# Seven block products instead of eight in the first products of two fused ffn layers

## The chip, the cores and the metric

The kernel runs on one core of one Trainium2 chip. The time is that of the whole kernel on the device, in microseconds; the median of three runs before the change is 671.86 us (671.8 to 671.88).

## The reference

Three blocks follow each other, all in float32 on arrays that are given in wider types where they are weights (64-bit, read as two 32-bit words):

```python
q_pool = q.reshape(B, H, S // 2, 2, D).mean(axis=3)        # B=2, H=8, S=1152, D=64
scores = (1 / sqrt(D)) * q_pool @ k.T
attn   = softmax(scores)
x      = (attn @ v) as [B * 576, 512]                       # 1152 tokens of 512
h = x @ w_in1                                               # 512 -> 2048
g = where(h >= 1, h, where(h <= -1, 0, (h + 1)**2 / 4))
x = g @ w_out1                                              # 2048 -> 512
h = x @ w_in2;  g = h * sigmoid(h);  out = g @ w_out2       # the second layer, same sizes
```

## The kernel before, in words

**Precision.** Every matrix that TensorE multiplies is split into a high part (rounded to fp32r) and a low part (what is left). A product of two such matrices is three matmuls: high x high, high x low, low x high. ScalarE makes the high parts with a copy; `lo_of` (L145) subtracts them for the low parts, nearly always on GpSimd (POOL).

**Weights.** `weight_tasks` (L85) loads a tile of 128 x 512 weights over SyncE's queue (SP) and turns its two words into float32 in five stages: `size` (L110, ScalarE), then `clamp` (L115), `shift` (L119), `sign` (L123) and `rest` (L127) on VectorE (DVE). All stages work in SBUF, on the tile `wf`, except for the first eight tiles, which are converted during attention by way of a PSUM bank. Then ScalarE copies the high part and GpSimd subtracts the low part.

**Ffn.** The 16 tiles of 128 hidden features of a layer are taken in groups of four (`GF`), the 1152 tokens in three blocks of 384 (`TB`). A step is one feature tile and one token block; there are 48 steps in a layer. `gemm1` (L158) makes the hidden values of a step: 4 chunks of 128 of x, three matmuls each, 12 matmuls of 384 columns, into one of four banks. Layer one: VectorE clips (L178), ScalarE squares (L184), VectorE takes the maximum (L188). Layer two: ScalarE's sigmoid (L180), then VectorE multiplies (L188). ScalarE copies the high part `gh` (L194), GpSimd makes the low part `gl`. `gemm2` (L202) multiplies by the output weights three steps later (`AHEAD`): in layer one 12 matmuls of 384 columns (L210), in layer two 9 of 512 (L212). Four banks add up the four tiles of a group. `keep` (L218) then takes a bank out: ScalarE copies it for the first group, VectorE adds it to `part` (L224) for the others. After the last group of layer one `part_hi` and `part_lo` split the sums for layer two; after that of layer two they are stored.

**The order.** Nothing is scheduled by a compiler. Every operation is an `op` with a target time, a list of engines with an estimate of how long it takes (occupied, and until its result is there), what it depends on, and the buffers that it needs. `plan_out` (L281) plays this through and always issues, on the engine that can start first, the operation that can start first; equal ones by target time. Targets are moved by a random amount (`SEED`, `SPREAD`). The program order of each engine comes from there and is fixed then. `both=True` marks VectorE operations that the planner keeps apart from GpSimd's. Attention's operations, the first eight weight tiles and the first steps of the ffn are in the same plan, so that ffn matmuls fill the end of attention.

Of the kernel before, what the change touches and what calls it, by code (L numbers as in the profile page):

```python
# [19 lines left out]
def fused_kernel(  # L20
# [16 lines left out]
    P = 128  # L37
# [7 lines left out]
    GF = 4  # L45
    NG = NF // GF
    FG = GF * P
    SC = S // 3
    RAWS, EARLY_RAWS = 4, 2
# [8 lines left out]
    SEED, SPREAD = 10, 1.0  # L58
    AHEAD = 3.0
# [3 lines left out]
    WPACE = 1.5  # L63
# [18 lines left out]
    seq = [(layer, g) for layer in range(2) for g in range(NG)]  # L82
    wt = {}

    def weight_tasks(idx, kind, pools, RAWS, via):  # L85


        layer, g = seq[idx]
        src = (((w_in1, w_out1), (w_in2, w_out2))[layer])["io".index(kind)]
        raws, parts = pools  # L90

        def quarter(c):
            st = {}

            def load():
                if c == 0:
                    wt[layer, g, kind] = [
                        parts.tile([P, 4, 512], F32R, tag=f"w{x}{kind}", name=f"w{x}{kind}") for x in "hl"
                    ]
                if kind == "i":  # L100
                    sv = src[c * P : (c + 1) * P, g * FG * 2 : (g + 1) * FG * 2]
                else:
                    sv = src[g * FG + c * P : g * FG + (c + 1) * P, :]
                raw = raws.tile([P, 512, 2], U32, tag="wr", name="wr", bufs=RAWS)
                nc.sync.dma_start(out=raw.rearrange("p f w -> p (f w)"), in_=sv)
                st["low"], st["top"] = raw[:, :, 0], raw[:, :, 1]

            def size():
                st["w"] = raws.tile([P, 512], F32, tag="wf", name="wf", bufs=RAWS)
                nc.scalar.activation(st["w"], st["top"].bitcast(F32), AF.Abs)  # L110

            def clamp():

                st["x"] = via[c]() if c in via else st["w"]
                nc.vector.tensor_scalar(st["x"], st["w"], LEAST, MOST, ALU.max, ALU.min)  # L115

            def shift():
                xi = st["x"].bitcast(U32)
                nc.vector.tensor_scalar(xi, xi, 3, 0x3FFFFFF8, ALU.logical_shift_left, ALU.bitwise_and)  # L119

            def sign():
                xi = st["x"].bitcast(U32)
                nc.vector.scalar_tensor_tensor(xi, st["top"], 0xC0000000, xi, ALU.bitwise_and, ALU.bitwise_or)  # L123

            def rest():
                wi, xi = st["w"].bitcast(U32), st["x"].bitcast(U32)
                nc.vector.scalar_tensor_tensor(wi, st["low"], 29, xi, ALU.logical_shift_right, ALU.bitwise_or)  # L127

            def parts_of():
                hi, lo = wt[layer, g, kind]  # L130
                nc.scalar.copy(hi[:, c], st["w"])
                lo_of(nc.gpsimd, lo[:, c], st["w"], hi[:, c])

            def part_hi():
                nc.scalar.copy(wt[layer, g, kind][0][:, c], st["w"])  # L135

            def part_lo():
                lo_of(nc.gpsimd, wt[layer, g, kind][1][:, c], st["w"], wt[layer, g, kind][0][:, c])

            return load, size, clamp, shift, sign, rest, parts_of, part_hi, part_lo  # L140

        return [quarter(c) for c in range(4)]
# [3 lines left out]

# [5 lines left out]
    TB = 384  # L152
    NB = NT // TB
    steps = [(layer, g, tb, j) for layer, g in seq for tb in range(NB) for j in range(GF)]
    hps, gg = {}, {}
    act = None

    def gemm1(i, ps, half):  # L158

        layer, g, tb, j = steps[i]  # L160
        wh, wl = wt[layer, g, "i"]
        ts_ = slice(tb * TB, (tb + 1) * TB)
        for c in range(half * ND // 2, (half + 1) * ND // 2):
            for n, (w, a) in enumerate(((wh, xh), (wh, xl), (wl, xh))):
                nc.tensor.matmul(  # L165
                    ps,
                    lhsT=w[:, c, j * P : (j + 1) * P],
                    rhs=a[:, c, ts_],
                    start=(c == 0 and n == 0),
                    stop=(c == ND - 1 and n == 2),  # L170
                )
        hps[i] = ps

    def act_a(i):
        gf = act.tile([P, TB], F32, tag="gf", name="gf")
        gg[i] = gf
        if steps[i][0] == 0:
            nc.vector.tensor_scalar(gf, hps[i], -1.0, 1.0, ALU.max, ALU.min)  # L178
        else:
            nc.scalar.activation(gf, hps[i], AF.Sigmoid)  # L180

    def act_b(i):
        if steps[i][0] == 0:
            nc.scalar.activation(gg[i], gg[i], AF.Square, bias=0.5, scale=0.5)  # L184

    def act_c(i):
        gf = gg[i]
        nc.vector.tensor_tensor(gf, hps.pop(i), gf, op=ALU.mult if steps[i][0] else ALU.max)  # L188

    def act_d(i):  # L190
        gf = gg[i]
# [5 lines left out]
    def act_e(i):  # L197
        gh, gl, gf = gg[i]
        lo_of(nc.gpsimd, gl, gf, gh)
        gg[i] = (gh, gl)  # L200
# [36 lines left out]

    part1 = part2 = None

    booked = []
# [758 lines left out]
```

## Time and profile before

| | |
|---|---|
| median of the runs | 671.86 us |
| the profiled execution's own time | 672.01 us |
| its span, first to last instruction | 670.2 us |
| TensorE busy (PE) | 663.2 us, 99% |
| weight loads of TensorE (PEld) | 619.9 us, 92% |
| VectorE (DVE) | 514.5 us, 77% |
| GpSimd (POOL) | 435.9 us, 65% |
| ScalarE (ACT) | 419.1 us, 63% |
| granted TensorE clock | 0.999 |

A share is a mean over three stretches that differ: attention to about 260 us, layer one to about 468 us, layer two to the end. Ends of matmuls are modelled and overlap with the next start; the distance between starts is what a matmul takes in a row.

### The profile page before, as it was taken

To read this page: it belongs to the slowest core of one execution; us is meant where nothing else is said; L and a number is where in the kernel's file an instruction comes from. 1 tells how busy PE (TensorE), PEld (TensorE's weight loads), DVE (VectorE), ACT (ScalarE), POOL (GpSimd) and SP (SyncE) were. 2 spreads that over 40 slices of the span, in tenths; PEclk is the share of its full clock that TensorE was granted. 3 is DMA by queue.
4 is the path that set the end of the run, shared out by engine and by line. 5 is a ranking of instruction groups with operands and counts; after the bars stand their busy time and mean duration, and the time that the engine had idled before them with its cause. 6 is when DMAs were issued, how large, how long until landed. Compare 5 with 4: busy or idle time off the path is not lost.

```text
span 670.2 us, 11784 instructions
## 1 busy us (share of the span) xinstructions
PE 663.2 (99%) x3962; PEld 619.9 (92%) x3962; DVE 514.5 (77%) x1184; ACT 419.1 (63%) x808; POOL 435.9 (65%) x413
## 2 busy tenths in 40 slices
PE   8999999999999999999999999999999999999997
PEld 7899998999899989999999999999999998989996
DVE  7888989898988897388898987886873684983223
ACT  6989998989999887455635543545554543432221
POOL 5888998989899689455645553576763653553121
PEclk9999999999999999999999999999999999999999
DMA  8967676666544455114233232221232231200012
GB/s 250 293 203 226 204 195 198 207 206 200 180 144 155 161 190 172 60 64 127 94 125 97 96 119 69 95 74 56 100 117 60 98 95 50 103 5 0 1 48 94
DMA packets 55292, 84.29 MB, mean 126 GB/s; under 512 B 14784, under 2 KB 32832, under 8 KB 55232
## 3 DMA queue, kind: packets, MB, share of 16 engines
q1 hardware_dynamic: 54656, 83.12, 39.5%
q8 instruction: 31, 0.51, 0.3%
q10 hardware_dynamic: 576, 0.43, 0.2%
q14 instruction: 29, 0.24, 0.1%
HBM read 49.81 MB, written 2.39 MB: 78 GB/s over the span
## 4 chain that ended last, share of the span: by engine, by line
PE 93%; DVE 4%; ACT 1%; issue 1%; DMA 1%; ACTq 0%; DVEq 0%
PE bank L165 30%; PE bank L210 15%; PE bank L212 15%; PE bank L613 11%; PE bank L690 10%; PE bank L677 5%; PE bank L732 2%; DVE p L620 2%; PE bank L673 2%; PE bank L501 1%; PE bank L719 1%; PE bank L537 1%; DMA kraw<-in_k_dram 1%; DVE thl L652 0%; DVE part L224 0%
## 5 line engine op out<-in xcount | busy, mean ns | idle before, releaser
L145 POOL TENSOR_TENSOR gl<-gf,gh 128x384 fp32r<-128x384 f32 x96 | 108.9, 1136 | 122.4 <-ACT gh L194 111.0
L165 PE MATMUL bank<-xh,whi 128*128 128x384 f32 x384 | 129.7, 338 | 0.0
L165 PE MATMUL bank<-xl,whi 128*128 128x384 f32 x384 | 129.2, 336 | 0.0
L165 PE MATMUL bank<-xh,wli 128*128 128x384 f32 x384 | 129.2, 336 | 0.0
L620 DVE TENSOR_SCALAR_CACHE_REDUCE p<-bank 128x384 f32<-128x384 f32 x192 | 102.1, 552 | 15.2 <-PE bank L613 11.4
L690 PE MATMUL bank<-thl,vhl 128*128 128x512 f32 x288 | 109.7, 421 | 0.0
L188 DVE TENSOR_TENSOR gf<-bank,gf 128x384 f32<-128x384 f32 x96 | 53.0, 552 | 73.7 <-ACT gf L180 69.2
L145 POOL TENSOR_TENSOR thl<-pf,thl 128x512 fp32r<-128x512 f32 x80 | 103.1, 1295 | 1.6
L613 PE MATMUL bank<-kk,qm 128*128 128x384 f32 x384 | 95.8, 352 | 0.4
L633 ACT ACTIVATE p<-p,low 128x1152 f32<-128x1152 f32 x64 | 81.4, 1273 | 2.6 <-DVE low L630 2.2
L194 ACT CAST gh<-gf 128x384 fp32r<-128x384 f32 x96 | 49.4, 514 | 48.4 <-DVE gf L188 42.7
L180 ACT ACTIVATE gf<-bank 128x384 f32<-128x384 f32 x48 | 23.6, 491 | 82.5 <-PE bank L165 81.3
L165 PEld LDWEIGHTS bank<-xh,whi 128*128 128x128 f32 x384 | 72.1, 188 | 3.1
L165 PEld LDWEIGHTS bank<-xl,whi 128*128 128x128 f32 x384 | 72.1, 188 | 3.0
L165 PEld LDWEIGHTS bank<-xh,wli 128*128 128x128 f32 x384 | 72.1, 188 | 0.0
L613 PEld LDWEIGHTS bank<-kk,qm 128*128 128x128 f32 x384 | 65.3, 189 | 5.5 <-DVE thl L652 0.5
L145 POOL TENSOR_TENSOR wlo<-wf,who 128x512 fp32r<-128x512 f32 x32 | 44.0, 1376 | 37.8 <-ACT who L135 34.5
L210 PE MATMUL bank<-gh,who 128*128 128x384 f32 x192 | 65.0, 339 | 0.0
L210 PE MATMUL bank<-gh,wlo 128*128 128x384 f32 x192 | 64.9, 338 | 0.0
L210 PE MATMUL bank<-gl,who 128*128 128x384 f32 x192 | 64.8, 337 | 0.0
L145 POOL TENSOR_TENSOR wli<-wf,whi 128x512 fp32r<-128x512 f32 x32 | 44.2, 1382 | 30.4 <-ACT whi L135 30.3
L652 DVE TENSOR_TENSOR thl<-bank,thl 128x512 fp32r<-128x512 f32 (+1 forms) x88 | 56.4, 649 | 4.9 <-ACT thl L651 4.2
(98 smaller groups left out, 1542.7 us busy)
## 6 DMA issues: line engine op xcount, KB each, us to landing
pr<-p SPq DMA_DIRECT2D x64, 256.0 KB, 2.8
wr<-in_moe_w_in_dram SPq DMA_DIRECT2D x32, 512.0 KB, 3.7
wr<-in_moe_w_out_dram SPq DMA_DIRECT2D x32, 512.0 KB, 3.3
pr<-p SPq DMA_DIRECT2D x64, 192.0 KB, 2.7
vraw<-in_v_dram SPq DMA_DIRECT2D x16, 288.0 KB, 3.0
kraw<-in_k_dram SPq DMA_DIRECT2D x15, 288.0 KB, 3.9
qraw<-in_q_dram SPq DMA_DIRECT2D x15, 256.0 KB, 3.9
rb<-row SPq DMA_DIRECT2D x16, 128.0 KB, 3.3
```

Source lines behind the costliest of these rows:

```text
L145: eng.tensor_sub(out, whole, hi.bitcast(F32))
L165: nc.tensor.matmul(ps, lhsT=w[:, c, j * P : (j + 1) * P], rhs=a[:, c, ts_], start=(c == 0 and n == 0), stop=(c == ND - 1 and n == 2),)
L188: nc.vector.tensor_tensor(gf, hps.pop(i), gf, op=ALU.mult if steps[i][0] else ALU.max)
L194: nc.scalar.copy(gh, gf)
L210: nc.tensor.matmul(ps[:, :TB], lhsT=w[:, j, m * P : (m + 1) * P], rhs=a, start=start, stop=stop)
L212: nc.tensor.matmul(ps[:, cols], lhsT=a[:, m * P : (m + 1) * P], rhs=w[:, j, cols], start=start, stop=stop)
L613: nc.tensor.matmul(ps, lhsT=qq[:, c0 : c0 + P], rhs=rhs, start=n == 0, stop=n == last)
L620: nc.vector.tensor_scalar(dst, ps, -1.0, None, ALU.mult, ALU.min, accum_out=mxs[key, t][:, j : j + 1])
L633: nc.scalar.activation(pt(), pt(), AF.Exp, bias=lows[key][:, tt : tt + 1], scale=-1.0, accum_out=sums[key][:, tt : tt + 1])
L652: o2 = op(target + 0.3, ("DVE", 0.6 * f, 0.683 * f, lambda: nc.vector.tensor_sub(tl(), ps(), th().bitcast(F32))), [o1], [bank, tb])
L677: nc.tensor.transpose(banks[bank.slot][:, i * P : (i + 1) * P].bitcast(F32R), prs[x][:, i, (c - COPIED[x][0]) * P : (c + 1 - COPIED[x][0]) ...
L690: nc.tensor.matmul(banks[yb.slot], lhsT=lhsT, rhs=thls[tb.slot][i], start=not count, stop=len(count) == 2 * KC - 1)
```

## The change

The whole ffn is written anew, with the same precision. Feature tiles are taken in 8 pairs `p` per layer, tokens in two blocks `SB`: 512 tokens in halves of 256, and 640 in halves of 320. A unit is a layer, a pair and a block. In the units of `PLAIN` (pairs 0 to 3 and 7 of layer one, 0 to 2 of layer two) the first product is made as before, in 24 matmuls of 512 columns or 48 of 320. In the other 8 pairs the product of a 2 x 2 block matrix of weights (two halves of x's features by the two tiles) and a 2 x 2 block matrix of x (two halves of its features by the two halves of the tokens) is made with seven products of six matmuls each instead of eight.

For that, weights need four more blocks, sums and differences of theirs (`combine`, on VectorE, 128 columns each, for each of the two loaded halves) with high and low parts of their own, and x needs four differences per token block and layer (`differences`). Where two products go to one sum, the second is added to the first in its PSUM bank (`start` is set for products 1, 6 and 5 alone): products 1 and 2 in bank 6, products 6, 7 and 4 in bank 4, products 5 and 3 in bank 5. VectorE takes sums out of the banks in between (five additions per unit), ScalarE copies twice; a product that adds to a bank waits until the bank was read (`reads`). Of these units the activation then works from SBUF, over both halves at once. The low parts `gl` of the hidden values are on GpSimd alone.

Weights are loaded and converted in the same number of tiles. The later stages of a conversion now go by way of PSUM bank 7 (`shift`, `sign`, `rest`); `clamp` stays in SBUF. Banks 0 to 3 add up the second products; where two units in a row share a token block, four of the block's keys (column tiles) are added over both and taken out once. In the last unit the keys are closed one after the other. Random shifts of targets have another seed, and a smaller width after attention.

```diff
...
-    SEED, SPREAD = 10, 1.0
-    AHEAD = 3.0
+    SEED, LATE_SEED, SPREAD, LATE_SPREAD = 24, 4, 1.0, 0.3
+    NP = NF // 2
+    SB = ((0, 256), (512, 320))
+    PLAIN = tuple((l, p, sb) for l in range(2) for p in range(NP) for sb in range(2) if (l, p) not in ((0, 4), (0, 5), (0, 6), (1, 3), (1, 4), (1, 5), (1, 6), (1, 7)))
+    LAG, LAGS = 1.2, {(0, 7): 0.0}
+    LEAD, RAW_I = 22, 2
+    TWINS, SHARED = ((0,0),(1,0)), ((1,0),)
...
+    def stages(raw, wf, bank, far):
+        low, top = raw[:, :, 0], raw[:, :, 1]
+        u = lambda x: x.bitcast(U32)
+        def size():
+            nc.scalar.activation(wf, top.bitcast(F32), AF.Abs)
+        def clamp():
+            nc.vector.tensor_scalar(bank if far else wf, wf, LEAST, MOST, ALU.max, ALU.min)
+        def shift():
+            nc.vector.tensor_scalar(u(bank), u(bank if far else wf), 3, 0x3FFFFFF8, ALU.logical_shift_left, ALU.bitwise_and)
+        def sign():
+            nc.vector.scalar_tensor_tensor(u(bank), top, 0xC0000000, u(bank), ALU.bitwise_and, ALU.bitwise_or)
+        def rest():
+            nc.vector.scalar_tensor_tensor(u(wf), low, 29, u(bank), ALU.logical_shift_right, ALU.bitwise_or)
+        return size, clamp, shift, sign, rest
...
+            rnd, late = Random(SEED), Random(LATE_SEED)
+            for n, o in enumerate(ops):
+                r = rnd if n < count else late
+                o.target += r.uniform(-SPREAD, SPREAD) * (1.0 if n < count else LATE_SPREAD)
...
+            flat = limit == 2 and not far
+            bank = None if flat else Buf("b") if far else Buf("b", want=7)
...
+            o = op(target, ("ACT", 0.57, 0.672, f(0)), [o], [raw])
+            if far:
+                o = op(target + 0.3, ("DVE", 0.6, 0.69, f(1)), [o], [raw, bank])
+            else:
+                o = op(target + 0.3, ("DVE", 0.332, 0.42, f(1)), [o], [raw], both=True)
+            for m in (2, 3, 4):
+                way = ("DVE", 0.335, 0.427) if flat and m == 2 else ("DVE", 0.6, 0.69)
+                o = op(target + 0.3 * m, (*way, f(m)), [o], [raw] if flat else [raw, bank], both=flat)
...
+                def combine(m, e, sf=sf, wf=wf):
+                    w, s = wf().rearrange("p (b n) -> p b n", n=P), at_(sf)
+                    add, sub = e.tensor_add, e.tensor_sub
+                    if m == 0:
+                        add(s[:, 0], w[:, 1], w[:, 3])
+                    elif m == 1:
+                        sub(s[:, 1], s[:, 0], w[:, 0])
+                    elif m == 2:
+                        sub(s[:, 2], w[:, 0], w[:, 1])
                     else:
...
+                        sub(s[:, 3], w[:, 2], s[:, 1])
+                for m in range(4):
+                    f = lambda e, m=m, c=combine: lambda: c(m, e)
+                    o = op(t + 1.8, [("DVE", 0.2, 0.29, f(nc.vector))], [o, *then], [raw, sf], both=True)
...
+        units = []
+        for layer in range(2):
+            p, last = 0, 1
+            while p < NP:
+                some = [p, p + 1] if (layer, p) in TWINS else [p]
+                first = last if p else 1 - last
+                units += [(layer, x, sb) for sb in (first, 1 - first) for x in some]
+                p, last = p + len(some), 1 - first
...
+            for m, (n, needs, a, b) in enumerate(((0, None, (0, 1), (0, 0)), (1, 0, (1, 1), None), (3, 1, (1, 0), None), (2, None, (1, 1), (0, 1)))):
+                steps = [("tensor_sub", n, (None, *a), b and (None, *b))]
+                if layer == 0:
+                    steps = [("tensor_sub", n, (xh, *a), b and (xh, *b)), ("tensor_add", n, None, (xl, *a)), ("tensor_sub", n, None, b and (xl, *b))]
...
+        def product(wb, block, rhs, ps, first):
+            wh, wl = at_(wb)
+            mh, ml = rhs
+            for i in range(2):
+                for n, (w, a) in enumerate(((wh, mh), (wh, ml), (wl, mh))):
+                    nc.tensor.matmul(ps, lhsT=w[:, i, block], rhs=a[:, i], start=first and i == n == 0, stop=i == 1 and n == 2, skip_group_check=not first)
...
+                what = [(0, "B11"), (2, "B21"), (7, "B22"), (3, "T4"), (4, "T1"), (5, "T2"), (6, "T3")]
+                size = 6 * MM[w]
+                o_c, reads = {}, {}
+                held = [Buf("b", want=6), Buf("b", want=4), Buf("b", want=5)]
+                for k, (m, x, dst, src) in enumerate(((1, 0, (0, 0), None), (6, 1, (0, 1), (0, 0)), (5, 2, None, None), (7, 1, (1, 1), (0, 0)), (2, 0, None, None), (4, 1, (1, 0), (0, 0)), (3, 2, (0, 1), (0, 1)))):
+                    bank = held[x]
+                    block, rhs = what[m - 1]
+                    tk = t + span * k / 7
+                    first = m in (1, 6, 5)
+                    go = lambda bank=bank, block=block, rhs=rhs, first=first: product(wb, block, blocks_of(u, rhs), bank_of(bank)[:, :w], first)
+                    o = after("PE", op(tk, ("PE", size, size + 0.165, go), [*deps, before.get("PE"), reads.get(x)], [bank, wb]))
+                    def add(dst, src, x, o, *needs, tk=tk):
+                        f = lambda: nc.vector.tensor_add(h_of(*dst), bank_of(held[x])[:, :w], h_of(*src))
+                        o_c[dst] = reads[x] = op(tk + size, ("DVE", *dve(w), f), [o, o_c[src], *needs], [held[x], hb[dst[0]], hb[src[0]]])
+                    if m == 1:
+                        f = lambda: nc.scalar.copy(h_of(0, 0), bank_of(held[0])[:, :w])
+                        o_c[0, 0] = reads[0] = op(tk + size, ("ACT", *act(w), f), [o], [held[0], hb[0]])
+                    elif m == 5:
+                        fifth = o
+                    elif m == 2:
+                        second_ = o
+                    else:
+                        add(dst, src, x, o)
+                        if m == 7:
+                            add((1, 1), (1, 1), 2, fifth)
+                f = lambda: nc.scalar.copy(h_of(0, 0), bank_of(held[0])[:, :w])
+                o_c[0, 0] = op(t + span, ("ACT", *act(w), f), [second_, o_c[1, 0]], [held[0], hb[0]])
+                ready = [[o_c[0, 0], o_c[0, 1]], [o_c[1, 0], o_c[1, 1]]]
...
+                        f = lambda s=s, hh=hh: nc.vector.scalar_tensor_tensor(hh(), s(), 1.0, hh(), ALU.min, ALU.max)
+                    else:
+                        o = op(t1, ("ACT", *act(n2), lambda s=s, hh=hh: nc.scalar.activation(s(), hh(), AF.Sigmoid)), ready[jj], bufs)
+                        f = lambda s=s, hh=hh: nc.vector.tensor_mul(hh(), hh(), s())
+                    o = op(t1 + 1, ("DVE", *dve(n2), f), [o], bufs, both=True)
...
+                ways = [("POOL", *pool_(n2), f)]
+                if True:
+                    if False: ways = [("DVE", *dve(n2), lambda gh=gh, gl=gl, hh=hh: lo_of(nc.vector, gl(), hh(), gh()))]
...
+            joined = n - 1 in opens
+            joins = same(n + 1) and not joined
+            if joins:
+                opens.add(n)
+            keys = keys_of[layer][sb]
+            shared = keys[-4:]
+            solo = keys[:-4]
+            final = n + 1 == len(units)
+            lots = [shared, solo] if joined else [solo, shared]
+            if final:
+                lots = [[k] for k in keys]
...
+                        closes = jj == 1 and not (joins and key in shared)
...
```

## Rows read from the trace of the kernel before

**Rows 1.** The profile's page, busy time, share and instructions.
```profile
PE 663.2 (99%) x3962; PEld 619.9 (92%) x3962; DVE 514.5 (77%) x1184; ACT 419.1 (63%) x808; POOL 435.9 (65%) x413
```

**Rows 2.** Busy time by stretch; PE, PEld, DVE, ACT, POOL, clock, DMA share, GB/s.
```profile
20.00:260.00 240.00, 239.24 (x1683) 219.07 (x1682) 212.59 (x683) 222.18 (x433) 215.46 (x218) 1.00 0.63 195
273.50:468.00 194.50, 194.49 (x1109) 194.13 (x1108) 162.40 (x257) 95.98 (x181) 106.53 (x87) 1.00 0.28 87
468.00:650.00 182.00, 182.00 (x914) 164.77 (x913) 110.36 (x160) 75.91 (x146) 86.67 (x72) 1.00 0.19 63
...
300.00:350.00 50.00, 49.99 (x286) 49.68 (x285) 45.55 (x70) 26.58 (x51) 27.71 (x23) 1.00 0.33 106
```

**Rows 3.** Longest wait of TensorE: total us, times, longest.
```profile
PE bank L426 <- POOL thl L408: 1.5, 1, 1.5
```

**Rows 4.** Timeline of TensorE in layer one: start, duration, instruction.
```profile
401.15 0.34 PE L210 MATMUL bank<-gh,who 128*128 128x384 f32 x1
...
403.27 0.34 PE L165 MATMUL bank<-xh,whi 128*128 128x384 f32 x1
...
405.38 0.34 PE L210 MATMUL bank<-gh,who 128*128 128x384 f32 x1
```

**Rows 5.** Chain that ended last, in layer two: start, us, what.
```profile
625.34 2.09 PE bank L165 x12
627.43 2.10 PE bank L212 x9
```

**Rows 6.** Timeline of the end, all engines (q is an issue).
```profile
664.95 2.17 DVE L224 TENSOR_TENSOR part<-bank,part 128x512 f32<-128x512 f32 x4 [3.78 <-PE bank L212]
...
665.46 0.28 PE L212 MATMUL bank<-who,gh 128*128 128x256 f32 x1
...
665.58 0.28 PE L212 MATMUL bank<-who,gl 128*128 128x256 f32 x1
...
666.05 0.28 PE L212 MATMUL bank<-wlo,gh 128*128 128x256 f32 x1
667.16 0.35 ACTq L236 DMA_DIRECT2D out_dram<-part  x1
```

**Rows 7.** Timeline of VectorE in layer two.
```profile
655.04 0.55 DVE L188 TENSOR_TENSOR gf<-bank,gf 128x384 f32<-128x384 f32 x1
655.50 1.28 DVE L224 TENSOR_TENSOR part<-bank,part 128x512 f32<-128x512 f32 x2
```

**Rows 8.** VectorE by line and shape, whole span: busy, mean ns | idle before.
```profile
L123 DVE SCALAR_TENSOR_TENSOR wf<-wr,wf 128x512 uint32<-128x512 uint32 x56 | 55.8, 996 | 0.7
...
L127 DVE SCALAR_TENSOR_TENSOR wf<-wr,wf 128x512 uint32<-128x512 uint32 x56 | 54.3, 970 | 0.7
...
L119 DVE TENSOR_SCALAR wf<-wf 128x512 uint32<-128x512 uint32 x56 | 37.5, 669 | 0.6
L115 DVE TENSOR_SCALAR wf<-wf 128x512 f32<-128x512 f32 x56 | 37.1, 663 | 1.2 <-ACT wf L110 1.1
...
L224 DVE TENSOR_TENSOR part<-bank,part 128x384 f32<-128x384 f32 x36 | 18.6, 547 | 1.2 <-PE bank L210 1.2
L224 DVE TENSOR_TENSOR part<-bank,part 128x512 f32<-128x512 f32 x26 | 17.6, 688 | 15.8 <-PE bank L212 15.7
...
L123 DVE SCALAR_TENSOR_TENSOR bank<-wr,bank 128x512 uint32<-128x512 uint32 x8 | 5.5, 688 | 0.0
L127 DVE SCALAR_TENSOR_TENSOR wf<-wr,bank 128x512 uint32<-128x512 uint32 x8 | 5.5, 683 | 0.1
...
L224 DVE TENSOR_TENSOR part<-bank,part 128x256 f32<-128x256 f32 x2 | 0.8, 421 | 0.0
```

**Rows 9.** GpSimd by line and shape, 300 to 400 us.
```profile
L145 POOL TENSOR_TENSOR gl<-gf,gh 128x384 fp32r<-128x384 f32 x24 | 28.8, 1199 | 21.5 <-ACT gh L194 13.1 <-issue 8.2
L145 POOL TENSOR_TENSOR wlo<-wf,who 128x512 fp32r<-128x512 f32 x10 | 14.3, 1427 | 11.5 <-ACT who L135 11.5
L145 POOL TENSOR_TENSOR wli<-wf,whi 128x512 fp32r<-128x512 f32 x10 | 14.2, 1424 | 11.9 <-ACT whi L135 11.9
```

More of the change, by code (lines that the diff above doesn't have):

```diff
@@ L79, in fused_kernel @@
     xl = const.tile([P, ND, NT], F32R, name="xl")
-    seq = [(layer, g) for layer in range(2) for g in range(NG)]
     wt = {}
[L85 to L142, printed above, removed]
@@ L151, in fused_kernel @@
     wpre = ctx.enter_context(tc.tile_pool(name="wpre", bufs=1, side="right"))
[L152 to L188, printed above, removed]
@@ L249, in __init__, with fits @@
             if due is not None:
                 booked.append(self)
+        def fits(self, have):
+            return [x for x in have if x[1] < self.limit and self.want in (None, x[1])]
     class Op:
@@ L255, in __init__ @@
             self.at = self.done = None
+            self.quick, self.behind = False, None
     ops = []
@@ L302, in admit @@
                 e = w[0]
[L303 removed]
+                t = max((d.next if d.by == e == "PE" or d is o.behind else d.done + handing(d.by if d.done > OPENED else "PE", e) for d in o.deps), default=0.0)
                 ready[e][id(o)] = (o, k, t)
@@ new lines, in fused_kernel, with at_, dve @@
+        for x, n in (("h", 3), ("s", 1), ("gh", 2), ("gl", 2)):
+            STAGE[x] = (n, late_act, late_rest)
+        called = set()
+        def at_(b):
+            if b.group in STAGE:
+                n, first, then = STAGE[b.group]
+                for f in (first, then if b.slot >= n else None):
+                    if f and f not in called:
+                        called.add(f)
+                        f()
+            return opened[b.group][b.slot]
+        def dve(n):
+            return 0.07 + n / 960, 0.155 + n / 960
@@ new lines, in last_of @@
+        def last_of(n, sb):
+            return not any(u[0] == units[n][0] and u[2] == sb for u in units[n + 1 :])
+        counts, opens = {}, set()
+        waiting_ = None
+        for n, u in enumerate(units):
+            if u[0] == 1 and units[n - 1][0] == 0:
+                second(n - 1, units[n - 1], waiting_)
+                waiting_ = None
+                x_ready = {sb: [o for _, o in outs[sb]] for sb in range(2)}
+                for sb in sorted(range(2), key=lambda sb: needed(1, sb)):
+                    t_ready[sb] = differences(1, sb, starts[needed(1, sb)] - 14, x_ready[sb])
+            hid = hidden(n, u)
+            if waiting_ is not None:
+                second(n - 1, units[n - 1], waiting_)
+            waiting_ = hid
@@ L965, in fused_kernel @@
+        second(len(units) - 1, units[-1], waiting_)
+        order = plan_out(len(attention))
         if REPORT:
```

553 lines of the change are left out of this document (377 added, 176 removed).

## The prediction

> **What bounds the kernel now.** I read the engines' busy times first, then the stretches, then what TensorE waited for, then its instructions one by one. The reader is to see that TensorE is busy for 99% of the span [rows 1]. The span has three parts: attention to about 260 us, the first ffn layer to about 468, the second to the end. In both layers TensorE has no gap at all (194.49 of 194.50 us, 182.00 of 182.00), at full clock [rows 2], and over the whole span its longest wait is the 1.5 us at the start [rows 3]. Busy time of matmuls is modelled and overlaps, so the price of a matmul is the distance between starts. Twelve of 384 columns take 2.12 and 2.11 us in layer one [rows 4], 0.176 us each; in layer two twelve take 2.09 and nine of 512 columns 2.10 us [rows 5], 0.174 and 0.233. So the ffn is a row of matmuls without holes, and only two things count: how many columns the change takes out, and whether the other engines still keep up.
>
> VectorE is next: 162.4 of 194.5 us in layer one and 45.55 of 50 in a stretch of it, against 106.5 for GpSimd and 96.0 for ScalarE [rows 2]. In layer two it has room (110.4 of 182).
>
> **TensorE's part.** Before, a pair of ffn tiles is six steps of 24 matmuls in layer one (6 x 4.23 = 25.4 us [rows 4]) and six of 12 + 9 in layer two (6 x 4.19 = 25.1 [rows 5]): 8 x 25.4 + 8 x 25.1 = 404.0 us.
>
> After, tokens are cut into 512 and 640 and halves of 256 and 320. A matmul of 256 columns stands in the trace at the end alone: six starts from 665.46 to 666.05, 0.118 us each [rows 6]. 320 columns do not stand there; between 0.118 (256) and 0.233 (512) the line gives 0.147. A plain pair has 24 matmuls of 512 and 48 of 320 columns in its first product: 24 x 0.233 + 48 x 0.147 = 12.7 us, the same in its second product in layer one, and 54 x 0.233 = 12.6 in layer two. A seven-product pair has 7 x 6 = 42 matmuls of 256 and 42 of 320: 42 x (0.118 + 0.147) = 11.1. Layer one has five plain pairs and three of seven products: 5 x 25.3 + 3 x 23.8 = 198.0. Layer two has three and five: 3 x 25.3 + 5 x 23.7 = 194.4. The sum is 392.4, so **TensorE needs 11.6 us less**. If 256 columns cost 0.129 in a long row instead, 8 x 42 x 0.011 = 3.7 of this is lost; I take 0.118, since it is a row of this very form.
>
> **VectorE's part**, which decides how much of this is kept. Its instructions follow each other 0.08 to 0.10 us before the last one's end: a 0.55 us one starts 0.46 before the next, and two of 0.69 take 1.28 [rows 7]. So I count the duration less 0.08.
>
> Weight conversion, four tiles per pair. Two-input instructions with both inputs in SBUF last 0.996 and 0.970 us, the same ones with one input in a PSUM bank 0.688 and 0.683 [rows 8]. The change puts shift, sign and rest on PSUM bank 7 and leaves only the clamp in SBUF (0.663), so a tile costs 0.66 + 3 x 0.69 less 4 x 0.08 = 2.4 instead of 0.996 + 0.970 + 0.669 + 0.663 less 0.32 = 3.0 us: 9.6 per pair instead of 12.
>
> Added in a seven-product pair:
> - Eight sums of 128-column weight blocks. None is in the trace; the additions of 512, 384 and 256 columns last 0.688, 0.547 and 0.421 [rows 8], a line that gives 0.29 for 128, so 8 x 0.21 = 1.7. Both inputs are in SBUF: with the 0.31 by which such instructions were longer above, 4.2.
> - Five additions from PSUM per unit: 5 x (0.42 - 0.08) + 5 x (0.49 - 0.08) = 3.7.
> - The activation's last step, four times over 512 or 640 columns, both inputs in SBUF: 2 x 0.92 + 2 x 1.05 = 3.9; without waiting 2.7.
>
> Sums kept from PSUM: in layer one 16 of 512 and 52 of 320 columns over eight pairs, (16 x 0.61 + 52 x 0.41) / 8 = 3.9; in layer two 44 of 512, 3.4; 3.6 us per pair. Together 9.6 + 1.7 + 3.7 + 3.9 + 3.6 = **22.5 us, and 25.0 when every block sum waits**; 21.3 when nothing waits. TensorE needs 23.8. So cover and bound are of one size. Before, VectorE ran 91% full over 50 us with no gap on TensorE, which speaks for the lower half; the products' order, in which an addition must be done before the next product may enter its bank, speaks for the upper. I take a stall of 0.45 us per pair for seven pairs (beside the last no weights are converted): **+3.2 us**, with bounds 0 and 7 x 1.2 = 8.4.
>
> The longer instructions above are those that share something with GpSimd. [...]
>
> **The rest.** Differences of x for the seven products: 20 VectorE instructions and 8 low parts in layer one, 28 x 0.98 = 27 us; they lie beside four plain pairs, whose VectorE work is 9.6 for weights, 2.9 for activations and 3.9 for sums, 16.4 of 25.3, so 36 us are free. In layer two it is 16 x 0.98 = 16 in three pairs with 27 free. Cost nothing, as long as they are issued early.
>
> GpSimd alone makes the low parts: 1.20 us for 384 and 1.43 for 512 columns [rows 9], by the line 1.66 for 640. A seven-product pair has 2 x 1.43 + 2 x 1.66 for the activations, 4 x 1.43 for weights, 2 x 1.43 for their sums: 14.8 of 23.8 us. It fits; nothing. ScalarE was half idle [rows 2] and gets two sums' high parts more; nothing.
>
> Between the layers and at the very end the order is coarser: a unit of 512 or 640 tokens must pass five steps (of about 0.5 us on ScalarE, 96 us / 181 [rows 2], 0.8 on VectorE, 1.66 on GpSimd, some 5 us in all) before its second product, and one unit's second product (5.6 us) covers them. Bounds 0 and 3 us; I take +1.3 for both places. Last additions: now four stand in a row (2.17 us from 664.95, with TensorE's last start at 666.05 and the last store issued at 667.16 [rows 6]); after, keys close one by one, and only the last addition is behind TensorE, -0.35. Weight loads and stores are as many as before on SP's queue, in the same order; nothing. In attention the order is drawn anew and other ffn work fills its end (24 matmuls of 512 before the last exponentials instead of 48 of 384, 2.8 us less, and as many more right after); VectorE, ScalarE and GpSimd are each near 90% there [rows 2]. I take 0, with one low part (1.4 us) either way.
>
> **Sum**, against the profiled execution's own 672.01 (span 670.2): 672.01 - 11.6 + 3.2 + 1.3 - 0.35 = 664.6. The median is 0.15 below this execution: **664.4 us**.
>
> **Rivals.**
> - *VectorE becomes the bound* in the seven-product pairs. Every two-input instruction meets a GpSimd low part, and with the products' waits a pair takes D us. Without stalls the time is 661.2; seven pairs add 7 x (D - 23.8). From D = 25.3 on it is slower than before; at D = 26 the time is 676.6. For: 25.0 is worked out above with the block sums alone waiting. Against: VectorE can slip weights into the plain pairs, and three of its four conversion steps leave SBUF. Chance 0.17.
> - *All hidden*: 22 us or less on VectorE, no stall: 661. For: at 91% nothing stalled before. Against: 22.5 is 95%. Chance 0.30.
> - *A wait in the products' own chain.* Seven products share three banks; the fourth, sixth and seventh wait for additions. Between a bank's product and its next lies one other (6 x 0.118 = 0.7 us in the small unit), against a 0.42 us addition and two handings over. If it fails by 0.2 us three times per unit, 16 x 0.6 = 9.6 us: 671, no change. Against: second products can be put between. Chance 0.12.
> - The forecast, 662.5 to 668.5: 0.41.
>
> **Chances and range.** About 0.2% (1.3 us) is what a measurement of this kernel tells from no change. Faster: 0.41 + 0.30 and some 0.04 of the third rival; slower: 0.16 of the first and 0.03 of the third; same: the rest, 0.06. The range goes from 659.5 (all hidden, a luckier attention) to 673.0, leaving out some 0.04 below and most of the first rival above; the forecast's own stands above.
>
> **What would show it.** In the profile after: starts of 256 and 320 columns 0.118 and 0.147 apart, or else the first term is wrong; 42 matmuls in either unit of a seven-product pair, where a plain one has 24 of 512 and 48 of 320 columns; TensorE without gaps in plain pairs; VectorE over 93% in the seven-product stretches, with small waits of TensorE on its additions there, some 3 us in all. Much longer ones, or VectorE at 99%, are the first rival; waits on the products' banks spread evenly over 16 units the third. Two-input conversion steps near 0.69 us show the move to bank 7 right. It is wrong altogether if the attention part differs by more than 2 us.

## The result: slower, where faster was forecast, and the profile after

The changed kernel takes 676.12 us (675.99 to 678.49, four runs) against 671.87 beside it: ratio 1.0072, interval 1.0049 to 1.0094. The forecast was 664.4 in a range of 659.5 to 673.0.

The profiled execution is the longest of the four, 678.49 us with a span of 676.7; the other three have spans of 674.2 to 674.4 and a higher mean clock (last section).

Busy time of the engines, as in [rows 1], and of three stretches, as in [rows 2] (PE, PEld, DVE, ACT, POOL, clock, DMA share, GB/s):

```profile
PE 658.3 (97%) x4058; PEld 594.3 (88%) x4058; DVE 582.1 (86%) x1346; ACT 456.3 (67%) x867; POOL 435.9 (64%) x386
```

```profile
20.00:260.00 240.00, 238.69 (x1661) 217.56 (x1661) 211.72 (x683) 221.81 (x431) 214.89 (x217) 1.00 0.63 197
280.00:380.00 100.00, 97.25 (x588) 90.94 (x587) 93.20 (x157) 61.72 (x121) 52.27 (x36) 0.98 0.24 74
...
460.00:550.00 90.00, 84.69 (x447) 73.68 (x446) 80.11 (x129) 49.41 (x92) 39.17 (x28) 0.98 0.22 71
```

VectorE (the third pair of numbers) has 68 us more to do in all and is 93% full in a stretch of mostly plain pairs of layer one, 89% in one of layer two. TensorE, which had not one gap in both layers before, now idles there. Its waits, where [rows 3] had only the start:

```profile
PE bank L1059 <- DVE h L1074: 4.8, 4, 2.4
PE bank L1187 <- DVE part L1219: 2.8, 3, 1.5
PE bank L1189 <- DVE part L1219: 2.1, 1, 2.1
PE bank L363 <- POOL thl L345: 1.5, 1, 1.5
```

L1059 is a plain first product, L1187 and L1189 second products of layers one and two: they wait for VectorE to empty a bank (L1219) or to finish a plain activation (L1074). The seven products (L1022) wait 0.9 us in all.

The price of a matmul came as forecast. Starts of 320 columns are 0.147 us apart, of 256 columns 0.12:

```profile
500.85 0.31 PE L1059 MATMUL bank<-xh,wih 128*128 128x320 f32 x1
501.00 0.31 PE L1059 MATMUL bank<-xl,wih 128*128 128x320 f32 x1
501.14 0.31 PE L1059 MATMUL bank<-xh,wil 128*128 128x320 f32 x1
...
577.34 0.28 PE L1022 MATMUL bank<-th,wil 128*128 128x256 f32 x1
577.46 0.28 PE L1022 MATMUL bank<-th,wih 128*128 128x256 f32 x1
577.58 0.28 PE L1022 MATMUL bank<-tl,wih 128*128 128x256 f32 x1
```

From the starts of all matmuls the span can be taken apart: an ffn matmul counts for its spacing in a row (0.2315 us for 512 columns, 0.1755 for 384, 0.147 for 320, 0.1195 for 256); distances longer than that by over 0.3 us are stalls; what is left of the ffn's distances is small waits and half clock (of the 5.3 us after, 4.3 fall into three stretches at half clock, see the last section).

| us | before | after | difference | forecast |
|---|---|---|---|---|
| ffn matmuls at their spacing | 403.2 | 391.2 | -11.9 | -11.6 |
| stalls over 0.3 us | 0 | 12.6 | +12.6 | +4.5 |
| small waits and half clock | 1.2 | 5.3 | +4.1 | 0 |
| distances between attention's matmuls | 260.2 | 262.2 | +2.0 | 0 |
| last start to the end | 4.2 | 3.9 | -0.2 | -0.35 |
| first start | 1.5 | 1.5 | 0 | 0 |
| span | 670.2 | 676.7 | +6.5 | -7.4 |

The eleven stalls: 1.6 and 1.1 us at 329 and 331; 0.6 at 367; 0.6, 0.4, 0.7, 1.9 and 2.6 from 462 to 506; 2.2 and 0.4 at 580 and 582; 0.7 at 617. Only those of 367 and from 580 on, 3.8 us, lie in seven-product pairs. 8.8 us lie in plain pairs: 0.6 at 462, between the layers; 1.1 at 478 and 481, before layer two's first difference of x (483.6); and 7.1 at 329, 331, 493 and 506, where the differences are made. VectorE is busy there for 61.65 of 64 and 29.47 of 32 us:

```profile
282.00:346.00 64.00, 61.65 (x371) 58.11 (x370) 61.65 (x96) 41.10 (x83) 30.56 (x21) 0.97 0.24 76
484.00:516.00 32.00, 27.91 (x154) 25.33 (x153) 29.47 (x44) 14.95 (x28) 14.14 (x10) 0.95 0.25 82
```

What VectorE did at 329, while a second product waited for a bank (its timeline):

```profile
327.37 1.51 DVE L96 TENSOR_SCALAR wf<-wf 128x512 f32<-128x512 f32 x1
328.80 1.77 DVE L989 TENSOR_TENSOR tf<-tf,xl 128x512 f32<-128x512 f32 x1
330.49 0.48 DVE L1219 TENSOR_TENSOR part<-bank,part 128x320 f32<-128x320 f32 x1
```

A clamp (L96) and a difference (L989) stand ahead of the addition that empties the bank. Free, the clamp lasts 0.42 us and the difference 0.68; here they last 1.51 and 1.77, and end 0.28 and 0.55 us after a low part of GpSimd has ended:

```profile
326.88 1.72 POOL L110 TENSOR_TENSOR wol<-wf,woh 128x512 fp32r<-128x512 f32 x1 [4.16 <-PE bank L1187]
328.56 1.46 POOL L110 TENSOR_TENSOR gl<-h,gh 128x512 fp32r<-128x512 f32 x1
```

The planner keeps clamps apart from GpSimd's work by its estimates alone: of the 56 clamps of the changed kernel 23 last over 0.5 us, and each of them ends 0.28 or 0.29 us after the end of a low part. That alone doesn't make a stall: in the kernel before, without one stall, 20 of 56 were held up in this way, and its longest clamp took 1.51 us as well:

```profile
L115 DVE TENSOR_SCALAR wf<-wf x56: 410/421/1509, 286.0 to 598.6; 128x512 f32<-128x512 f32 x56
```

The figures are the shortest, the middle and the longest in ns. The same at 580: a clamp of 1.52 and a block sum of 1.62, in place of 0.28, ahead of L1219. At 506 nothing is prolonged, and the chain runs over ScalarE. TensorE waits from 506.3 on for an activation (L1074) that needs a sigmoid of ScalarE (L1072). The product was done at 505.0, but in ScalarE's order the high part of a difference (`th`) stands ahead of the sigmoid, and ScalarE idles for 2.74 us until VectorE has made that difference:

```profile
506.54 0.72 ACT L854 CAST th<-tf 128x640 fp32r<-128x640 f32 x1 [2.74 <-DVE tf L989]
507.17 0.61 ACT L854 CAST wih<-wf 128x512 fp32r<-128x512 f32 x1
507.69 0.43 ACT L1072 ACTIVATE s<-bank 128x320 f32<-128x320 f32 x1
```

VectorE meanwhile; only the last 0.2 us of the delay are its own, a low part ahead of L1074:

```profile
505.69 0.82 DVE L989 TENSOR_TENSOR tf<-part 128x640 f32<-128x640 f32 x1
506.42 0.28 DVE L889 TENSOR_TENSOR sf<-sf,wf 128x128 f32<-128x128 f32 x1
506.62 0.82 DVE L989 TENSOR_TENSOR tf<-part 128x640 f32<-128x640 f32 x1
507.36 0.28 DVE L891 TENSOR_TENSOR sf<-wf 128x128 f32<-128x128 f32 x1
507.56 0.82 DVE L110 TENSOR_TENSOR tl<-tf,th 128x640 fp32r<-128x640 f32 x1
508.30 0.48 DVE L1074 TENSOR_TENSOR h<-bank,s 128x320 f32<-128x320 f32 x1
```

At 493 both come together: a difference lasts 1.65 us in place of 0.68, its high part and then the sigmoid wait for it on ScalarE, and a conversion step and a low part stand ahead of L1074 on VectorE.

### The profile page after: what moved, and what is told of

Its sections match the earlier page's. It is cut to its first block, busy times and chain, and to the rows that moved or that the text cites. A ratio compares the mean times of both kernels' runs of the same rounds, so it can differ in the third digit from the quotient of the medians.

```text
span 676.7 us, 12151 instructions
## 1 busy us (share of the span) xinstructions
PE 658.3 (97%) x4058; PEld 594.3 (88%) x4058; DVE 582.1 (86%) x1346; ACT 456.3 (67%) x867; POOL 435.9 (64%) x386
## 4 chain that ended last, share of the span: by engine, by line
PE 76%; DVE 16%; issue 3%; DMA 2%; ACT 2%; SPq 0%; DVEq 0%; ACTq 0%
PE bank L1187 12%; PE bank L1189 11%; PE bank L1022 11%; PE bank L1059 10%; PE bank L550 10%; PE bank L627 9%; PE bank L614 5%; PE bank L669 2%; DVE wf L96 2%; DVE bank L102 2%; DVE p L557 2%; PE bank L610 2%; DMA pr<-p 1%; DVE tf L989 1%; DVE part L1219 1%
## 5 line engine op out<-in xcount | busy, mean ns | idle before, releaser
L110 POOL TENSOR_TENSOR gl<-h,gh 128x512 fp32r<-128x512 f32 (+1 forms) x64 | 95.8, 1503 | 62.3 <-ACT gh L1128 43.8
L557 DVE TENSOR_SCALAR_CACHE_REDUCE p<-bank 128x384 f32<-128x384 f32 x192 | 101.6, 552 | 14.9 <-PE bank L550 12.6
L1059 PE MATMUL bank<-xh,wih 128*128 128x320 f32 (+1 forms) x192 | 66.5, 346 | 4.8 <-DVE h L1074 4.8
L1187 PE MATMUL bank<-gh,woh 128*128 128x320 f32 (+1 forms) x192 | 65.2, 339 | 2.8 <-DVE part L1219 2.8
L1219 DVE TENSOR_TENSOR part<-bank,part 128x512 f32<-128x512 f32 (+1 forms) x90 | 51.9, 586 | 16.7 <-PE bank L1189 8.4
L1059 PE MATMUL bank<-xl,wih 128*128 128x320 f32 (+1 forms) x192 | 65.9, 343 | 0.0
L1059 PE MATMUL bank<-xh,wil 128*128 128x320 f32 (+1 forms) x192 | 65.6, 342 | 0.0
L1187 PE MATMUL bank<-gh,wol 128*128 128x320 f32 (+1 forms) x192 | 65.0, 339 | 0.0
L1187 PE MATMUL bank<-gl,woh 128*128 128x320 f32 (+1 forms) x192 | 65.0, 338 | 0.0
L1189 PE MATMUL bank<-woh,gh 128*128 128x512 f32 (+1 forms) x145 | 57.6, 397 | 2.1 <-DVE part L1219 2.1
L1189 PE MATMUL bank<-woh,gl 128*128 128x512 f32 (+1 forms) x145 | 57.1, 394 | 0.0
L1189 PE MATMUL bank<-wol,gh 128*128 128x512 f32 (+1 forms) x145 | 57.1, 394 | 0.0
```

The costliest lines, as they stand in the source:

```text
L110: eng.tensor_sub(out, whole, hi.bitcast(F32))
L557: nc.vector.tensor_scalar(dst, ps, -1.0, None, ALU.mult, ALU.min, accum_out=mxs[key, t][:, j : j + 1])
L1059: nc.tensor.matmul(bank_of(bank)[:, : a1 - a0], lhsT=lhsT, rhs=a, start=c == k == 0, stop=c == ND - 1 and k == 2)
L1187: nc.tensor.matmul(bank_of(ab)[:, :cw], lhsT=b[:, m * P : (m + 1) * P], rhs=a[:, c0 : c0 + cw], start=start and k == 0, stop=stop)
L1189: nc.tensor.matmul(bank_of(ab)[:, cols], lhsT=a[:, c0 : c0 + cw], rhs=b[:, cols], start=start and k == 0 and cols.start == 0, stop=stop an ...
L1219: f = lambda dst=dst, ab=ab, size=size: nc.vector.tensor_add(dst(), bank_of(ab)[:, :size], dst())
```

## The experiments

Three theories. A: VectorE's instructions with all inputs in SBUF wait for GpSimd's low parts, and what is urgent waits behind them. B: VectorE simply has too much to do in these stretches. C: the drawn order is unlucky. Every edit but that of run 5 (and the repeat, run 9) is planned anew and so has another order too; the draws of runs 7 and 10 show what that alone can do, up to 8 us. Ratios are against the kernel before on the same chip; its median was 672.97 beside the first four, 672.89 beside the next four, 672.59 beside the last. "Stalls" are counted as in the table.

**1. One difference instead of four.**

```diff
...
-for m, (n, needs, a, b) in enumerate(((0, None, (0, 1), (0, 0)), (1, 0, (1, 1), None), (3, 1, (1, 0), None), (2, None, (1, 1), (0, 1)))):
+for m, (n, needs, a, b) in enumerate(((0, None, (0, 1), (0, 0)),)):
...
-            return opened["tt"][sb][int(rhs[1]) - 1]
+            return opened["tt"][sb][0]
```

> Leaves out three of the four differences of x per token block and layer (the first stands in for all four), so that VectorE has 6 instead of 20 of them and 2 instead of 8 low parts in layer one, 2 instead of 8 and 2 instead of 8 in layer two; all seven products stay. Theory A (VectorE's instructions with inputs in SBUF alone wait for a GpSimd low part, and a late addition queued behind them holds TensorE): the stalls at 329 to 331 and 462 to 506 us (8.8 us and two drops of the clock) go, 664 to 668 us. Theory B (VectorE has simply too much work there, blocked or not): the same, 664 to 668. Theory C (the drawn order happens to put urgent VectorE work behind other work; a new draw moves the stalls but does not remove them): 672 to 678.

Measured 667.55 us, ratio 0.993 (0.9912 to 0.9948); stalls 5.3, clock 1.0. Those around 330 are gone, of those from 458 to 506 two are left (3.0). The longer, 2.4 us at 488, comes with the one difference that is still made in layer two for these tokens: it lasts 1.79 us beside a low part, and its high part stands ahead of the sigmoid on ScalarE. That fits the differences as the cause. Their price is not shown by this run: it gains 1.4% on the changed kernel by the ratios, and another draw alone gained 1.2%. A and B are not told apart.

**2. The differences on GpSimd.**

```diff
-ways = [("DVE", *dve(2 * w), f(nc.vector))]
+ways = [("POOL", *pool_(2 * w), f(nc.gpsimd))]
...
-lambda tt=tt: tt(1), 2 * w, [o_t[n]], [tb[n]], True))
+lambda tt=tt: tt(1), 2 * w, [o_t[n]], [tb[n]]))
```

> The differences of x and their low parts are made by GpSimd instead of VectorE (28 instructions in layer one, 16 in layer two, about 1.5 us each, so GpSimd gets some 65 us more and VectorE 43 us less). Theory B (load): the stalls in the plain stretches go, 664 to 668. Theory A (GpSimd low parts block VectorE): GpSimd is busy longer, so clamps and block sums wait oftener; half of it is kept, 667 to 673. Theory C: 672 to 678.

Measured 672.82, ratio 1.0002 (0.9993 to 1.0012); stalls 7.0. VectorE is busy for 71 of 100 us from 280 to 380 and GpSimd for 86. The stalls in plain pairs fall from 8.8 to 1.6 us, as B had it; but 5.4 us lie in seven-product pairs now (3.8 before), the longest 2.9 us at 381. There the addition that TensorE waits for starts at 383.42 behind eight VectorE instructions in a row, none of them prolonged: a queue, and not a low part in the way. The time is at the edge of A's range and above B's, so neither is decided.

**3. The clamp by way of PSUM bank 7.** It lasts 0.685 us there on the mean, so VectorE has as much to do as before the edit (93.8 of 100 us from 280 to 380).

```diff
-            if far:
+            if not flat:
                 o = op(target + 0.3, ("DVE", 0.6, 0.69, f(1)), [o], [raw, bank])
...
-            f = lambda m: lambda: stages(*pair(), pair()[1] if flat else bank_of(bank), far)[m]()
+            f = lambda m: lambda: stages(*pair(), pair()[1] if flat else bank_of(bank), not flat)[m]()
```

> The clamp of a weight conversion writes to PSUM bank 7 too, as it does in the first eight tiles, so that it lasts 0.69 us without waiting (now 0.775 on the mean, 0.42 to 1.79). VectorE's load stays the same within 5 us over the whole ffn. Theory A: the waits of 1 us and more of 56 clamps are gone, and with them about half of the stalls: 668 to 672. Theory B: no change, 674 to 678. Theory C: 672 to 678.

Measured 667.95, ratio 0.9931 (0.9916 to 0.9946); stalls 4.1. Its stretches and clamps:

```profile
280.00:380.00 100.00, 99.23 (x619) 93.69 (x618) 93.77 (x163) 64.78 (x126) 54.80 (x38) 1.00 0.28 86
...
460.00:550.00 90.00, 88.71 (x477) 77.38 (x476) 80.63 (x137) 49.79 (x92) 42.97 (x31) 1.00 0.23 72
```

```profile
L96 DVE TENSOR_SCALAR bank<-wf 128x512 f32<-128x512 f32 x62 | 42.5, 685 | 9.2 <-ACT wf L93 8.8
```

VectorE is as full, TensorE idles 2.1 us in these two stretches where it idled 8.1. For A, at the lower edge of its range, and against B; but the order was planned anew, which C allows.

**4. Low parts of hidden values by either engine.**

```diff
-                    if False: ways = [("DVE", *dve(n2), lambda gh=gh, gl=gl, hh=hh: lo_of(nc.vector, gl(), hh(), gh()))]
+                    ways += [("DVE", *dve(n2), lambda gh=gh, gl=gl, hh=hh: lo_of(nc.vector, gl(), hh(), gh()))]
```

> Undoes the part of the change by which low parts of the hidden values are on GpSimd alone: the planner may give one to VectorE when VectorE has nothing urgent. Theory A: a few long GpSimd instructions fewer, each taken when VectorE is idle, 673 to 677. Theory B: VectorE gets more work, 676 to 682. Theory C: 672 to 678.

Measured 676.25, ratio 1.0051 (1.0034 to 1.0068); stalls 12.2. The planner gives 63 of the 64 low parts to VectorE, not a few. GpSimd's work from 280 to 380 falls from 52 to 28 us, VectorE's rises to 97 of 100, and nothing is won. "GpSimd alone" is not what costs. Only 3 clamps last over 1 us, where 18 did, but low parts that VectorE makes are held up in their place: one that lasts 1.5 to 1.6 us beside a low part of GpSimd, and 0.5 to 0.8 when free, stands ahead of each of the three largest stalls (at 471 one of x, 1.6 us; at 576 and 603 one of the hidden values, 2.4 and 1.5 us). That is A's mechanism on other instructions, with more work for VectorE as B has it. All three ranges hold 676.25, so the time decides nothing.

**5. The clamp kept in SBUF in another form, every engine's order unchanged.**

```diff
...
-            nc.vector.tensor_scalar(bank if far else wf, wf, LEAST, MOST, ALU.max, ALU.min)
+            nc.vector.tensor_scalar(bank, wf, LEAST, MOST, ALU.max, ALU.min) if far else nc.vector.tensor_scalar(wf, wf, LEAST, None, ALU.max, ALU.min, accum_out=least)
```

> The changed kernel with every engine's instructions in exactly the order they have there; only the clamps of 56 weight tiles differ: still in SBUF, in the form that also writes out its smallest value (the one that attention's scores use), without the upper bound, which is left out. Each should take about 0.69 and 0.08 us, longer than the 0.42 us of an undisturbed clamp, but not wait for GpSimd. Theory A (blocked behind GpSimd's low parts): the stalls shrink although VectorE has 17 us more to do, 668 to 673. Theory B (load): more stalls, 678 to 684. Theory C (an unlucky order): the same order, so the same stalls, 675 to 678.

Measured 670.51, ratio 0.9968 (0.9957 to 0.998), against 1.0073 for the changed kernel itself (9, below): 1% less with the same order; stalls 7.4, clock 1.0. The clamps of the changed kernel and of this one:

```profile
L96 DVE TENSOR_SCALAR wf<-wf x56: 414/423/1793, 275.9 to 635.7; 128x512 f32<-128x512 f32 x56
```

```profile
L96 DVE TENSOR_SCALAR_CACHE_REDUCE wf<-wf 128x512 f32<-128x512 f32 x56 | 37.8, 676 | 2.4 <-ACT wf L93 2.4
...
L96 DVE DVE_READ_ACCUMULATOR wf<-wf 128x1 f32 x56 | 4.5, 80 | 0.0
```

Before the edit the shortest, middle and longest clamp last 414, 423 and 1793 ns, 43.4 us in all; after it each takes 0.68 and 0.08 us, 42.3 in all. The expectation of 17 us more was wrong: waits had already cost that much. The same total, and in both traces every engine runs the same instructions in the same order, only no clamp waits: A is shown for the clamps, worth about 7 us by the two ratios. The gain is all in layer two and in the clock. In layer one, where VectorE is busy for 97.34 of 100 us from 280 to 380, the stalls are as large as before (3.8 us, 3.2 in the changed kernel) and lie elsewhere; from 460 us on they fall from 9.4 to 3.7. So blocked clamps are not the whole cause.

**6. All pairs plain.**

```diff
-    PLAIN = tuple(... if (l, p) not in ((0, 4), (0, 5), (0, 6), (1, 3), (1, 4), (1, 5), (1, 6), (1, 7)))
+    PLAIN = tuple((l, p, sb) for l in range(2) for p in range(NP) for sb in range(2))
...
-        for sb in sorted(range(2), key=lambda sb: needed(0, sb)):
+        for sb in ():
...
```

> All 16 pairs plain: eight products, no block sums, no differences; all the rest of the rewriting stays. TensorE's part is 11.6 us longer than in the changed kernel. Theories A and B: hardly a stall is left, since the two-input VectorE work in SBUF is gone; 673 to 676. If the rewriting itself (units of 512 and 640 tokens, one bank for all conversions, joined sums) brought the stalls: 680 to 688.

Measured 673.24, ratio 1.0008 (0.9998 to 1.0017); stalls 0.6; ffn matmuls 402.6 us at their spacing. The rest of the rewriting costs and brings nothing that can be measured; the seven products bring 11.4 us and the stalls. Held-up clamps are there too (12 of 56 last over 1 us), and VectorE, busy for 66 of 100 us from 280 to 380, takes them with 0.6 us of stalls in all: here a held-up clamp costs nothing, since the queue behind it is short.

**7 to 11. Other draws, with the clamp in SBUF and in the bank, and the changed kernel once more.**

```diff
-    SEED, LATE_SEED, SPREAD, LATE_SPREAD = 24, 4, 1.0, 0.3
+    SEED, LATE_SEED, SPREAD, LATE_SPREAD = 24, 1, 1.0, 0.3
```

This is run 7. Run 8 has run 3's edit with it, runs 10 and 11 are the same two with 2 in place of 1, and run 9 has no edit.

> The changed kernel with another random draw of the targets after attention (seed 1 instead of 4), nothing else. Theories A and B: the stalls lie elsewhere but add up to much the same, 673 to 679. Theory C: the draw decides, anywhere from 665 to 680, and below 671 as likely as not.

> The clamp by way of PSUM bank 7 (as in the run with the clamp in the bank) with the same other draw. Theory A: again some 6 to 8 us below the changed kernel with this draw, 666 to 671. Theory C: no relation to the earlier gain, 665 to 680.

> The changed kernel once more, unchanged, beside the next three on one chip, to have its own scatter from chip to chip. All theories: 674 to 677, or 0.5 to 0.9% above the kernel before.

> The changed kernel with a third draw (seed 2). With draw 1 it was 669.1 against 676.1 with its own, so Theory C holds a share. If stalls come from the draw alone, this one is anywhere from 665 to 678; by theory A, which leaves the draw to decide only how many urgent instructions stand behind blocked ones, 668 to 676, and in every draw stalls over 5 us.

> The clamp by way of bank 7 with draw 2. Theory A: below the changed kernel with draw 2 by 2 to 8 us, as in the two other draws (8.1 and 2.6 us), 665 to 669, with stalls under 5 us. Theory C: no relation, 665 to 678.

| draw | clamp in SBUF (as changed) | stalls | clamp in bank 7 | stalls |
|---|---|---|---|---|
| 4 (its own) | 677.26, ratio 1.0073 (1.0057 to 1.009) | 12.2 | 667.95, 0.9931 | 4.1 |
| 1 | 669.12, 0.9952 (0.9936 to 0.9967) | 6.9 | 666.49, 0.9904 (0.9889 to 0.9919) | 3.3 |
| 2 | 672.51, 1.0004 (0.9992 to 1.0016) | 8.7 | 666.32, 0.9911 (0.9896 to 0.9926) | 4.9 |

The draw of the change is the worst of three, by up to 8 us: C holds that share, and I had expected 673 to 679 for draw 1 by A and B, wrongly. The draws also differ in how many clamps are caught: 18 of 56 last over 1 us with draw 4, 9 with draw 1, 11 with draw 2. With draw 1 the clamp in the bank gains 2.6 us and not 6 to 8, with draw 2 it gains 6.2. But every draw stalls by 6.9 us or more with the clamp in SBUF and by less than 5 with it in the bank, where the three lie within 1.6 us. With draw 1 or 2 and the clamp in the bank the kernel is 0.9 to 1.0% faster than the kernel before.

**12. All pairs plain, differences made and not used.**

```diff
-    PLAIN = tuple(... if (l, p) not in (...))
+    ONCE = tuple(... if (l, p) not in (...))
+    PLAIN = tuple((l, p, sb) for l in range(2) for p in range(NP) for sb in range(2))
...
-            return next(n for n, u in enumerate(units) if u[0] == layer and u[2] == sb and u not in PLAIN)
+            return next(n for n, u in enumerate(units) if u[0] == layer and u[2] == sb and u not in ONCE)
```

> All pairs plain (eight products), but the differences of x are made as in the changed kernel and then not used: 36 VectorE instructions with their low parts alone, put into the plain stretches of both layers. The prediction's own term (they cost nothing there): as all plain, 673 to 674, stalls under 1 us. Theory A: they block the plain activations and sums also without the seven products, stalls of 2 to 6 us at 300 to 340 and at 470 to 510 us, 675 to 679.

Measured 675.7, ratio 1.005 (1.0035 to 1.0065) against 1.0008 without them; stalls 2.5, one of them of 1.5 us at 504, at the same wait as in the changed kernel (its lines are one further down here):

```profile
PE bank L1060 <- DVE h L1075: 1.4, 1, 1.4
```

The trace has 28 differences and 16 low parts of them on VectorE, 44 instructions and not the 36 of the expectation. At 504 too the sigmoid stands behind a high part of a difference that ScalarE waits for, 0.9 us here, and then a difference and a low part stand ahead of the activation on VectorE, 0.9 us more. So differences alone can stall plain pairs: 2.8 us (0.4%) here, in layer two above all, in one draw, so that this price is not told apart from that of the new order. At 330 they do no harm by themselves (VectorE 88 of 100 us there, against 93 with the block sums and what belongs to the seven products); A's 2 to 6 us there did not come.

## Why the prediction was wrong

**TensorE's part held**: -11.9 where -11.6 was worked out (-12.1 when its sums are not rounded in between), with 256 and 320 columns at 0.12 and 0.147 us; the 0.129 that was weighed for 256 columns is not what the trace shows. So did the small term at the end.

**The step that failed first is that the differences of x "cost nothing, as long as they are issued early".** I compared sums, in layer one 27 us of work with 36 us free beside four plain pairs. They were issued early, and TensorE stalled for 7.1 us just where the differences of both layers are made. Two things were wrong. The free time is a mean over four pairs, some 100 us, while layer one's differences are all made within 64, where other work for the seven products lies too: VectorE has 2.4 us left there, waits for GpSimd counted as work. And each difference stands in two orders that are fixed, VectorE's and ScalarE's, ahead of an activation or an addition that TensorE waits for: at 506 the sigmoid waits for a difference it has nothing to do with. One difference instead of four took the stalls around 330 away (with a new order), and differences alone go with 2.8 us more in a kernel without seven products.

**The stall term was mis-sized and put in the wrong place.** 3.2 us in the seven-product pairs, bounds 0 to 8.4, and 1.3 at the boundaries were forecast; 12.6 were measured, 3.8 of them in those pairs. I had taken VectorE at its mean (22.5 to 25.0 us per pair) and the clamp at its mean of 0.66. The middle clamp lasts 0.42 and the longest 1.79: 33 of 56 are free, the others wait for a GpSimd low part, and in a full queue a stall comes behind the long ones. In the kernel before it was so already (0.42 and 1.51), hidden in the mean that I read. The longer conversion steps there, which the prediction put down to GpSimd, were waits for its low parts too: of the 56 sign steps in SBUF 31 last 0.67 to 0.69 us, as the eight with one input in a bank do (0.68 to 0.69), and the other 25 last 0.85 to 1.83 and end 0.55 us after the end of a low part (shortest, middle and longest in ns):

```profile
L123 DVE SCALAR_TENSOR_TENSOR wf<-wr,wf x56: 674/693/1834, 288.6 to 604.2; 128x512 uint32<-128x512 uint32 x56
```

VectorE instructions held up in this way stand ahead of what TensorE waits for in three of the four largest stalls (329, 493, 580), and run 5 shows the price for the clamps with the order unchanged, about 7 us; the largest, at 506, is queueing alone, and so is the largest of run 2. That the conversion's last three steps would leave this behind was right: sign and rest now last 0.688 and 0.680 us where they lasted 0.996 and 0.970 [rows 8]:

```profile
L102 DVE SCALAR_TENSOR_TENSOR bank<-wr,bank 128x512 uint32<-128x512 uint32 x62 | 42.7, 688 | 0.7
L105 DVE SCALAR_TENSOR_TENSOR wf<-wr,bank 128x512 uint32<-128x512 uint32 x62 | 42.2, 680 | 0.8
...
L1125 DVE TENSOR_TENSOR h<-h,s 128x640 f32<-128x640 f32 x10 | 10.3, 1025 | 0.1
...
L889 DVE TENSOR_TENSOR sf<-sf,wf 128x128 f32<-128x128 f32 x16 | 9.0, 561 | 0.0
```

The block sums (one of four lines shown) last 0.47 us on the mean of all 64, between the 0.28 of a free one and the 0.60 of the upper bound; the activation's last step over 640 columns lasts 1.03, free 0.82, where 1.13 was taken.

**Missing altogether** was the half clock after three of the stalls: 4.1 us more of half clock and small waits, nearly all of it at a granted clock of 0.50.

**Attention** takes 2.0 us more, and 1.0 to 2.9 more in every kernel of this study that has the new ffn. I had allowed 1.4 and named more than 2 as a sign of being wrong; it is at that mark. Whether it is the new draw for attention or the other ffn work at its end was not tried and stays open.

**The rivals.** The first (VectorE the bound) has the right engine and sign, but not the right place: TensorE waits in plain pairs above all, not in the seven-product pairs whose D it priced. The second (all hidden) is out with 12.6 us of stalls. The third (the products' own chain) is out: L1022 waits 0.9 us in all. The draw, for which I had allowed nothing in the ffn, is worth up to 8 us.

## What to carry to other kernels

When work is put on an engine that has time left, ask what will stand in its queue ahead of which urgent instruction, and for how long at worst, and ask the same of the engine that works on its results; a load averaged over a longer stretch doesn't tell. Look at the longest duration of a line beside its middle one: a wide spread can be a wait for another engine, and an instruction that is a little slower but always takes the same time (here a clamp of 0.69 us into PSUM in place of one of 0.42 to 1.79) can be worth 1% of a kernel. And try several draws of a planned order before judging a change by one.

## What the runs showed of the hardware that was not expected

After three stalls TensorE ran at half clock for 3.4 us each, from 332.9, 510.4 and 582.0 us on. The first two rows below begin earlier, at full clock; from 332.9 to 336.2 and from 510.4 to 513.7 it is 0.50 too. In the last the granted clock is 0.50 throughout, and in the second, which starts at full clock, matmuls of 320 columns start 0.267 us apart, where it was 0.147:

```profile
331.40:336.20 4.80, 3.91 (x14) 3.26 (x13) 4.80 (x11) 2.67 (x5) 2.00 (x2) 0.65 0.10 16
508.80:513.50 4.70, 4.66 (x22) 4.66 (x23) 3.29 (x4) 1.79 (x3) 4.04 (x3) 0.67 0.57 225
582.10:585.20 3.10, 3.08 (x10) 2.77 (x11) 3.10 (x9) 0.62 (x1) 0.00 (x0) 0.50 0.00 0
```

```profile
512.04 0.47 PE L1059 MATMUL bank<-xl,wih 128*128 128x320 f32 x1
512.31 0.47 PE L1059 MATMUL bank<-xh,wil 128*128 128x320 f32 x1
512.58 0.47 PE L1059 MATMUL bank<-xh,wih 128*128 128x320 f32 x1
```

TensorE had stood for 1.6 and 1.1, for 2.6 and for 2.2 us before. Not every stall was followed by it. In the same profile it ran on at full clock after 1.9 us at 493; in run 9, the same program, after the 2.2 us at 580; in run 1 after 2.4 us. Other executions of the changed kernel have a mean clock of 0.996 or 0.997 in place of 0.992 and are 2.2 to 2.5 us shorter. By these clocks they spent about 5 us less at half clock, which is worth about half of that (0.267 against 0.147 us from start to start): an estimate that accounts for the spread between the four runs, though no trace of the other three is kept.
